# Taking early modes into x while the last weights load, and adding the late rows on two halves of the PE array

## Chip, cores, metric

The kernel runs on one core of a Trainium2 chip. Times are device microseconds (us) of that core, a median over executions. The profiler's span is about 2 us shorter than the time of the same execution, so spans are compared with spans and times with times. "Ratio" is the mean time of one kernel's fast runs over that of the other's fast runs of the same rounds, so it is not quite the ratio of the medians quoted.

## The reference, cut to what matters

An attention with forget gates gives x, of shape [8 batches, 576 rows, 512 columns]. Then comes a spectral mix:

```python
X = np.fft.rfft(x, axis=1)
# for the first 64 modes: complex weights, one 512 x 512 matrix per mode
Yr = einsum('bmd,mde->bme', Xr, w_r) - einsum('bmd,mde->bme', Xi, w_i)
Yi = einsum('bmd,mde->bme', Xr, w_i) + einsum('bmd,mde->bme', Xi, w_r)
y = np.fft.irfft(Y, n=576, axis=1)
u = x + y
out = u + np.maximum(u @ w_ch, 0.0)
```

The weights are 134 MB in DRAM, and loading them takes most of the time. y is an inverse transform: 128 numbers (64 modes, real and imaginary) per batch and column, times a fixed basis `BI`. Because the transform is linear, `u @ w_ch` can be built as `x @ w_ch` (called XW and computed while the weights load) plus the basis times `Y @ w_ch`.

## The kernel before

The weights come in tiles. The second half of the load uses tiles of 2 modes. The last 8 tiles that arrive hold the first 16 modes, so 32 of the 128 rows of Y are "late". After the last tile, each output job adds in PSUM, on PE: XW through an identity matrix, x also through the identity in jobs of type N, and the basis times `yy` (t=0 is Y, t=1 is `Y @ w_ch`) over all 128 rows.

```python
def emit_late(q4):     # late rows of four batches at once: 4 x 32 rows
    ... 4 transposes into ply, 4 matmuls with w_ch into plw
def emit_rows(b, pl):  # used for batch 0 only: straight to rows 0..31
    rows = slice(32 * (b % 4), 32 * (b % 4) + 32)
    nc.vector.tensor_copy(yy[0:32, b, 0, :], pl[0][rows, :])
    nc.scalar.copy(yy[0:32, b, 1, :], pl[1][rows, :])
def emit_late_rows(q4, pl):   # other batches: copy out, then move the rows by DMA
    nc.vector.tensor_copy(yl[:, 0, :], pl[0][:, :])
    nc.scalar.copy(yl[:, 1, :], pl[1][:, :])
    for j in range(1 - q4, 4):
        nc.sync.dma_start(yy[0:32, 4*q4 + j, :, :], yl[32*j : 32*j + 32, :, :])
def emit_x(job):       # identity matmuls: XW always, x for types N and Q
    for p, t in ((pu, x_all), (pz, XW)):
        if t is x_all and ty not in "NQ": continue
        for i in range(nb):
            nc.tensor.matmul(p[:, i, :], lhsT=ident_bf[:, :], rhs=t[...], start=True, stop=False)
def emit_out(job, ps, last):
    ... nc.tensor.matmul(p[:, i, :], lhsT=BI[:, block], rhs=yy[:, b, t, :])   # 128 rows
    # types N, Q: ACT copies pu out; P, W: DVE adds x to pu
    # types P, Q: ACT relu(pz), POOL adds; N, W: DVE max and add
    ... store
jobs = [(*j, ty) for j, ty in zip(jobs, "NPWPNPWPNNPWPNNPWNNN")]
```

There are 20 jobs: 16 of two 128-row blocks, and every fifth one (sb=4) of one block made of the last 64 rows of two batches. PSUM holds four tiles of two banks, and a job takes two of them (pu and pz).

The softmax here doesn't subtract the row's maximum and nothing guards it: scores larger than these inputs give would overflow.

Of the kernel before, what the change touches and what calls it, by code (L numbers as in the profile page):

```python
# [8 lines left out]
F32 = mybir.dt.float32  # L9
BF16 = mybir.dt.bfloat16  # L10
# [5 lines left out]
def _strided(ap: bass.AP, free_dims, offset_elems: int = 0) -> bass.AP:  # L16
    new_ap = [list(ap.ap[0])] + [list(x) for x in free_dims]
    return bass.AP(tensor=ap.tensor, offset=ap.offset + offset_elems, ap=new_ap)
# [3 lines left out]
def kernel(  # L22
# [11 lines left out]
    nc = tc.nc  # L34
    B, H, S, Dh = q.shape
    NM = moe_w_r.shape[0]
    D = H * Dh
# [4 lines left out]
    SP = NSB * 128  # L42
    NDC = D // 128
# [8 lines left out]
    def xi(b, sb):  # L52
        return (b % 2) * 3 + sb if sb < 3 else 6 + b % 2 if sb == 3 else 8
# [6 lines left out]
    const = ctx.enter_context(tc.tile_pool(name="const", bufs=1))  # L60
    xpool = ctx.enter_context(tc.tile_pool(name="xpool", bufs=1))
    wpool = ctx.enter_context(tc.tile_pool(name="wpool", bufs=NRING))
    xtpool = ctx.enter_context(tc.tile_pool(name="xtpool", bufs=3))
    x_all = xpool.tile([128, B // 2, NX, D], BF16, name="x_all")
    Yacc = xpool.tile([128, NDC, NM, 2 * B], F32, name="Yacc")
    late = {}
# [2 lines left out]
    wch = const.tile([128, NDC, D], BF16, name="wch")  # L69
    bas = const.tile([128, NSB + 1, NM, 2], BF16, name="bas")  # L70
    BI = const.tile([128, SP], BF16, name="BI")

    wtiles = {}

# [2 lines left out]
    NT = NDC * NG  # L77
    NTH = NT // 2
    M2 = MG // 2
    GL = 8  # L80

    def tile_of(n):
        if n < NTH:
# [33 lines left out]
    def emit_modes(n):  # L117
# [28 lines left out]
        if n < NG:  # L146
            nc.vector.tensor_copy(ysl, A[:, :, :, :])
        elif n < NTH:
            nc.vector.tensor_tensor(ysl, A[:, :, :, :], ysl, ALU.add)
        else:  # L150
            n8 = nm * 2
            yt, w = (late["YTl"], GL * n8) if g < GL else (late["YT"], 2 * NM)
            nc.vector.tensor_tensor(  # L153
                _strided(
                    yt[:, 0, 0, g * n8 : g * n8 + 1], [[B * w, NDC], [w, B], [1, n8]]
                ),
                _strided(A[:, 0, 0, 0:1], [[nm * 2 * B, NDC], [1, B], [B, n8]]),
                _strided(
                    Yacc[:, 0, g * nm, 0:1], [[NM * 2 * B, NDC], [1, B], [B, n8]]
                ),  # L160
                ALU.add,
            )

    with ExitStack() as actx:
# [191 lines left out]
        def emit_basis():  # L356
# [42 lines left out]
            for sc in range(NSB):  # L399
                bip = psT.tile([128, 128], F32, tag="tr", name="bip")  # L400
                nc.tensor.transpose(
                    bip[:, :],
                    Zt[:, sc, :, :].rearrange("p m ri -> p (m ri)"),
                    ident_f[:, :],
                )
                nc.vector.tensor_scalar(
                    BI[:, sc * 128 : (sc + 1) * 128], bip[:, :], coef[:], None, ALU.mult
                )


        QT, vaugs = {}, {}
# [177 lines left out]
        nmode = 0  # L589
# [41 lines left out]

    with ExitStack() as bctx:
        bsb = bctx.enter_context(tc.tile_pool(name="bsb", bufs=1))
        YT = bsb.tile([128, NDC, B, 2 * NM], BF16, name="YT")
        raw = xtpool.tile([128, NM, 3 * B], BF16, tag="XT3", name="YTl")
        nl = 2 * GL * M2
        YTl = (
            raw[:, :, :]
            .rearrange("p m c -> p (m c)")[:, 0 : NDC * B * nl]
            .rearrange("p (e b c) -> p e b c", e=NDC, b=B)  # L640
        )
        late["YT"], late["YTl"] = YT, YTl
        XW = bsb.tile([128, B // 2, NX, D], BF16, name="XW")
        yy = bsb.tile([128, B, 2, D], BF16, name="yy")
        nc.vector.memset(YT[:, :, :, 0 : 2 * GL * M2], 0.0)

        yflat = yy[:, :, :, :].rearrange("p b t e -> p (b t e)")
        xTs = [
            yflat[:, i * NDC * SP : (i + 1) * NDC * SP].rearrange(
                "p (e s) -> p e s", e=NDC  # L650
            )
            for i in range(3)
        ]

        with ExitStack() as cctx:
            late["psM"] = cctx.enter_context(
# [29 lines left out]
                        )  # L686
                    nc.scalar.copy(XW[:, bp, i0 + i, :], pxw[:, :])  # L687

            def emit_y(b):
                pyw = psBig.tile([128, D], F32, tag="big", name="pyw")  # L690
                for eb in range(NDC):
                    nc.tensor.matmul(  # L692
                        pyw[:, :],
                        lhsT=YT[:, eb, b, :],
                        rhs=wch[:, eb, :],
                        start=(eb == 0),
                        stop=(eb == NDC - 1),
                    )
                nc.scalar.copy(yy[:, b, 1, :], pyw[:, :])  # L699
                yp = psBig.tile([128, D], BF16, tag="big", name="yp")  # L700
                for eb in range(NDC):
                    nc.tensor.transpose(
                        yp[:, eb * 128 : (eb + 1) * 128], YT[:, eb, b, :], ident_bf[:, :]
                    )
                nc.vector.tensor_copy(yy[:, b, 0, :], yp[:, :])

            nx = ny = 0
            last = NT
            while nmode < last - 1:
                emit_modes(nmode)  # L710
                nmode += 1
                next_w()
                if nmode % 4 and nx < B:
                    emit_xw(nx)
                    nx += 1
                if nmode > last - 6 and ny < B - 1:
                    for _ in range(2 if ny < 4 else 1):
                        emit_y(ny)
                        ny += 1
            emit_y(ny)  # L720
            assert nx == B == ny + 1

        psZ = bctx.enter_context(
            tc.tile_pool(
# [3 lines left out]
        late["psM"], late["psZ"] = None, psZ  # L728


        def emit_late(q4):
            pl = psZ.tile([128, 2, D], F32, tag="z", name="pl")
            plw = pl[:, 0, :]
            ply = pl[:, 1, 0 : D // 2].bitcast(BF16)
            lhs = [
                YTl[:, eb, 4 * q4 : 4 * q4 + 4, :].rearrange("p b c -> p (b c)")
                for eb in range(NDC)
            ]
            for eb in range(NDC):
                nc.tensor.transpose(  # L740
                    ply[:, eb * 128 : (eb + 1) * 128], lhs[eb], ident_bf[:, :]
                )
            for eb in range(NDC):
                nc.tensor.matmul(
                    plw,
                    lhsT=lhs[eb],
                    rhs=wch[:, eb, :],
                    start=(eb == 0),
                    stop=(eb == NDC - 1),
                )  # L750
            return ply, plw

        yls = {}

        def emit_rows(b, pl):
            rows = slice(32 * (b % 4), 32 * (b % 4) + 32)
            nc.vector.tensor_copy(yy[0:32, b, 0, :], pl[0][rows, :])
            nc.scalar.copy(yy[0:32, b, 1, :], pl[1][rows, :])

        def emit_late_rows(q4, pl):  # L760
            yl = xtpool.tile([128, 2, D], BF16, tag="XT3", name="yl")
            nc.vector.tensor_copy(yl[:, 0, :], pl[0][:, :])
            nc.scalar.copy(yl[:, 1, :], pl[1][:, :])
            for j in range(1 - q4, 4):
                nc.sync.dma_start(
                    yy[0:32, 4 * q4 + j, :, :], yl[32 * j : 32 * j + 32, :, :]
                )

        def xblk(t, job):
            b, sb, nb, _ = job  # L770
# [21 lines left out]

        def emit_out(job, ps, last):
            b, sb, nb, ty = job
            for t, p in enumerate(ps):
                fresh = t == 0 and ty not in "NQ"
                for i in range(nb):
                    if sb == 4:
                        for h in range(2):
                            nc.tensor.matmul(  # L800
                                p[64 * h : 64 * h + 64, 0, :],
                                lhsT=BI[:, 512:576],
                                rhs=yy[:, b + h, t, :],
                                start=fresh,
                                stop=True,
                                skip_group_check=True,
                            )
                    else:
                        nc.tensor.matmul(
                            p[:, i, :],  # L810
                            lhsT=BI[:, (sb + i) * 128 : (sb + i + 1) * 128],
                            rhs=yy[:, b, t, :],
                            start=fresh,
                            stop=True,
                            skip_group_check=True,
                        )
            pu, pz = (p[:, 0:nb, :] for p in ps)
            uo = wpool.tile([128, 2, 2, D], F32, tag="wb", name="uo")
            u_sb, o_sb = uo[:, 0, 0:nb, :], uo[:, 1, 0:nb, :]
# [28 lines left out]
        for bp in range(B // 2):  # L848
            jobs += [(b, sb, 2) for b in (2 * bp, 2 * bp + 1) for sb in (0, 2)]
            jobs.append((2 * bp, 4, 1))  # L850
        jobs = [(*j, ty) for j, ty in zip(jobs, "NPWPNPWPNNPWPNNPWNNN")]
        ps0 = emit_x(jobs[0])
        emit_modes(nmode)
        pl = emit_late(0)
        emit_rows(0, pl)
        emit_late_rows(0, pl)
        for n, job in enumerate(jobs):
            emit_out(job, emit_x(job) if n else ps0, n == len(jobs) - 1)
            if n == 3:
                emit_late_rows(1, emit_late(1))  # L860
# [1 line left out]
_INS = ['q', 'k', 'v', 'f', 'moe_w_r', 'moe_w_i', 'moe_w_ch']  # L862
_OUTS = [((8, 576, 512), 'float32')]
# [25 lines left out]
```

## Time and profile before

| | before |
|---|---|
| time, median | 448.64 us (448.2 to 449.03), 3 runs |
| span of the profiled run | 446.5 us |
| last weights used | 405.34 us |
| tail after that | 41.2 us |

The strips of the page show each engine's busy share in 40 equal slices (in tenths), the clock granted to PE (in tenths), and the DMA share and rate.

```profile
PE   2388888989788788768597969999822238527993
...
PEclk9999999959599555897769578999955558856998
DMA  8999999999999999999999999999999999991698
GB/s 203 206 233 233 234 234 233 152 233 206 233 234 207 234 216 224 233 211 229 231 210 235 211 212 211 211 211 211 211 211 211 211 211 211 211 196 28 225 362 296
```

From about slice 26 the weight loads pace the kernel at 211 GB/s. PE has gaps there, and its clock is often at half. The last four slices are the tail.

The chain of waits gives the start of the tail. Its columns are start, duration, and what the chain went through.

```profile
405.34 0.56 PE A L138 x14
406.34 0.61 PE pl L740 x4
...
411.32 1.99 DMA yy<-yl
413.36 0.62 PE pu L809 x2
```

The last weights come at 405.34 us. The late rows follow. The DMA that moves them to other partitions takes 2 us from 411.32, and PE stands idle 1.4 us of it before the third job.

The next table is the tail by stage. Its columns are window, length, then busy time and count for PE, PE weight loads, DVE, ACT and POOL, then granted clock, DMA share and GB/s. The boundaries at 417, 424.2, 431.3 and 438.8 are close to the matmuls of the sb=4 jobs, so each of those stages is one group of five jobs.

```profile
core 0: us, PE busy (x) PEld busy (x) DVE busy (x) ACT busy (x) POOL busy (x), PEclk, DMA share, GB/s
406.30:408.90 2.60, 2.56 (x10) 1.18 (x11) 0.20 (x1) 0.00 (x0) 0.00 (x0) 0.50 0.00 0
408.90:412.50 3.60, 2.96 (x12) 0.95 (x10) 2.30 (x4) 3.00 (x4) 0.00 (x0) 1.00 0.00 0
412.50:417.00 4.50, 3.64 (x20) 1.71 (x20) 3.58 (x4) 1.03 (x1) 2.35 (x1) 1.00 0.57 201
417.00:424.20 7.20, 7.15 (x35) 2.86 (x36) 6.80 (x8) 4.03 (x5) 4.95 (x3) 1.00 0.64 232
424.20:431.30 7.10, 7.05 (x35) 2.77 (x34) 6.74 (x7) 3.54 (x4) 4.76 (x3) 1.00 0.97 347
431.30:438.80 7.50, 7.39 (x35) 2.96 (x34) 6.42 (x6) 3.37 (x4) 4.46 (x2) 1.00 0.99 368
438.80:446.50 7.70, 0.63 (x5) 0.14 (x4) 1.82 (x2) 0.85 (x2) 0.00 (x0) 0.77 0.73 275
```

A group takes 7.0 to 7.5 us with PE nearly full and DVE at 86 to 95%, and the DMA share is at 0.97 to 0.99 in the last two groups. The stage to 408.9 runs at half clock.

These PE lines of the timeline (start, busy time, line, operation) hold two durations that the costing needs.

```profile
416.61 0.38 PE L783 MATMUL pu<-x_all,ident_bf 128*128 128x512 bf16 x1
416.83 0.38 PE L783 MATMUL pz<-XW,ident_bf 128*128 128x512 bf16 x1
417.14 0.41 PE L800 MATMUL pu<-yy,BI 128*64 128x512 bf16 x2
417.38 0.38 PE L800 MATMUL pz<-yy,BI 128*64 128x512 bf16 x2
417.74 0.59 PE L783 MATMUL pz<-XW,ident_bf 128*128 128x512 bf16 x2
```

Full matmuls of 512 columns start 0.215 us apart. A job with sb=4 writes two halves of the columns of the array: a pair starts together (x2) and 0.24 us after the previous pair. From the full-array matmul at 416.83 to the first pair it is 0.31 us instead of 0.215, so about 0.09 us is added where the kind of tile changes. "Busy" in these lines is the pipelined length; the distance of the starts is what PE's time costs.

### The profile page before, as it was taken

What the parts mean: (1) busy time and instruction counts of PE and PEld (TensorE: products, weight loads), DVE (VectorE), ACT (ScalarE), POOL (GpSimd) and SP (SyncE); (2) the same over time, 40 slices, a digit from 0 to 9 for tenths busy, and PEclk for the clock granted to TensorE, in tenths of its full rate; (3) what the DMA queues carried; (4) which work ended last, traced back from release to release, by engine and by line L of the source; (5) the groups of instructions that cost most, each with busy time, mean ns of one, the idle gap of its engine ahead of it and who ended that gap; (6) DMA issues with size and microseconds to landing.
All of it is one profiled execution on the core that took longest, in us unless ns stands there. A gap on an engine that the chain in (4) does not pass through costs nothing.

```text
span 446.5 us, 11102 instructions
## 1 busy us (share of the span) xinstructions
PE 327.1 (73%) x4791; PEld 222.6 (50%) x4791; DVE 237.3 (53%) x602; ACT 202.4 (45%) x296; POOL 146.1 (33%) x194
## 2 busy tenths in 40 slices
PE   2388888989788788768597969999822238527993
PEld 1255555766566566556465746656612224323441
DVE  5768888776676546656377664223300002103894
ACT  3378888647567454664446533443200002102442
POOL 7333330534343323323333223232322323200661
PEclk9999999959599555897769578999955558856998
DMA  8999999999999999999999999999999999991698
GB/s 203 206 233 233 234 234 233 152 233 206 233 234 207 234 216 224 233 211 229 231 210 235 211 212 211 211 211 211 211 211 211 211 211 211 211 196 28 225 362 296
DMA packets 66431, 97.25 MB, mean 218 GB/s; under 512 B 3376, under 2 KB 44848, under 8 KB 66384
## 3 DMA queue, kind: packets, MB, share of 16 engines
q0 software_dynamic: 62480, 85.34, 103.3%
q1 hardware_dynamic: 3824, 11.09, 6.9%
q8 instruction: 37, 0.61, 0.5%
q10 hardware_dynamic: 80, 0.13, 0.1%
q14 instruction: 10, 0.08, 0.0%
HBM read 163.73 MB, written 9.44 MB: 388 GB/s over the span
## 4 chain that ended last, share of the span: by engine, by line
DMA 58%; PE 18%; DVE 7%; ACT 7%; issue 3%; POOL 1%; SPq 1%; DVEq 0%; ACTq 0%; POOLq 0%
DMA wb<-in_moe_w_i_dram 30%; DMA stk<-in_k_dram 13%; DMA stq<-in_q_dram 11%; ACT E L496 4%; DMA wb<-in_moe_w_r_dram 3%; PE tp L437 3%; PE pav L534 3%; PE pxw L680 3%; PE ps L489 3%; PE A L138 2%; DVE XT L581 2%; PE vp L461 1%; DVE uo L821 1%; PE ptr L669 1%; ACT KT L450 1%
## 5 line engine op out<-in xcount | busy, mean ns | idle before, releaser
L496 ACT ACTIVATE E<-ps 128x1024 bf16<-128x1024 f32 (+1 forms) x128 | 104.5, 859 | 39.3 <-PE ps L489 27.2
L138 PE MATMUL A<-XT,wb 128*128 128x16 bf16 x2048 | 71.6, 172 | 56.8 <-DMA wb<-in_moe_w_i_dram 35.0
L138 PEld LDWEIGHTS <-wb 128*128 128x128 bf16 x2048 | 64.0, 100 | 72.6 <-DMA wb<-in_moe_w_i_dram 38.2
L88 POOL DMA_DIRECT2D wb<-in_moe_w_r_dram x65 | 47.5, 731 | 134.7 <-PE A L138 30.4
L88 POOL DMA_DIRECT2D wb<-in_moe_w_i_dram x65 | 47.1, 725 | 78.2 <-DMA wb<-in_moe_w_i_dram 45.1
L489 PE MATMUL ps<-QTs,KT 64*128 64x64 bf16 (+4 forms) x384 | 57.5, 319 | 6.1 <-ACT E L496 5.9
L534 PE MATMUL pav<-va,E 128*128 128x65 bf16 (+1 forms) x1088 | 55.9, 210 | 4.3 <-DVE x_all L556 2.6
L534 PEld LDWEIGHTS <-E 128*128 128x128 bf16 (+1 forms) x1088 | 45.1, 114 | 15.8 <-issue 5.6
L153 DVE TENSOR_TENSOR YT<-A,Yacc 128x128 bf16<-128x128 f32 x24 | 8.9, 369 | 77.2 <-PE A L138 77.2
L511 DVE TENSOR_TENSOR E<-E,trimask 128x256 bf16<-128x256 bf16 (+2 forms) x128 | 38.2, 317 | 6.8 <-ACT E L496 6.4
L450 ACT COPY KT<-tp 128x640 bf16<-128x640 bf16 (+1 forms) x32 | 22.1, 745 | 26.6 <-PE tp L437 26.4
L687 ACT CAST XW<-pxw 128x512 bf16<-128x512 f32 x36 | 20.3, 587 | 29.8 <-PE pxw L680 25.1
L680 PE MATMUL pxw<-wch,yy 128*128 128x512 bf16 x144 | 33.5, 382 | 0.0
L699 ACT CAST yy<-pyw 128x512 bf16<-128x512 f32 x8 | 4.7, 586 | 60.7 <-PE pyw L692 60.7
L437 PE MATMUL tp<-ident_bf,kb 128*128 128x128 bf16 x144 | 16.1, 269 | 19.1 <-DVE kb L421 19.1
L556 DVE TENSOR_TENSOR x_all<-pav,rcp 128x384 bf16<-128x384 f32 x64 | 29.2, 456 | 0.9
L454 ACT COPY VT<-tp 128x640 bf16<-128x640 bf16 (+1 forms) x32 | 22.5, 753 | 12.6 <-PE tp L437 12.4
L489 PEld LDWEIGHTS <-KT 64*128 64x128 bf16 x384 | 18.1, 98 | 19.8 <-issue 11.6
L828 POOL TENSOR_TENSOR uo<-uo 128x1024 f32<-128x1024 f32 x7 | 16.5, 2359 | 29.3 <-DVE uo L821 25.5
L581 DVE CAST XT<-px 128x128 bf16<-128x128 f32 x32 | 21.0, 805 | 8.6 <-PE px L571 8.6
L425 DVE TENSOR_TENSOR vb<-stv,wdec 128x1152 bf16<-128x1152 f32 x16 | 21.6, 1351 | 5.4 <-PE tp L437 4.7
L452 DVE COPY QTs<-tp 128x640 bf16<-128x640 bf16 (+1 forms) x32 | 23.3, 767 | 0.8 <-PE tp L437 0.8
(108 smaller groups left out, 439.4 us busy)
## 6 DMA issues: line engine op xcount, KB each, us to landing
wb<-in_moe_w_r_dram POOLq DMA_DIRECT2D x63, 512.0 KB, 17.6
wb<-in_moe_w_i_dram POOLq DMA_DIRECT2D x63, 512.0 KB, 18.1
out_dram<-uo SPq DMA_DIRECT2D x16, 512.0 KB, 3.7
stv<-in_v_dram POOLq DMA_DIRECT2D x14, 576.0 KB, 15.6
stk<-in_k_dram POOLq DMA_DIRECT2D x16, 288.0 KB, 15.3
stq<-in_q_dram POOLq DMA_DIRECT2D x16, 288.0 KB, 15.3
stv<-in_v_dram SPq DMA_DIRECT2D x2, 576.0 KB, 6.1
out_dram<-uo SPq DMA_DIRECT2D x7, 128.0 KB, 3.9
```

Source lines behind the costliest of these rows:

```text
L88: tc.keep_in_program_order(nc.gpsimd.dma_start(dst, src))
L138: nc.tensor.matmul(A[:, eb, mi, :], lhsT=wb[:, t, mi, r * D + eb * 128 : r * D + (eb + 1) * 128], rhs=XT3[:, m, c0 : c0 + 2 * B], start=(i ...
L437: nc.tensor.transpose(tp[:, r - r0, :, :].rearrange("c h p -> c (h p)"), sb[:, r, :, :].rearrange("p b d -> p (b d)"), ident_bf[:, :],)
L450: nc.scalar.copy(rows(KTs[pr % 2][:, :, 0:S]), tv)
L452: nc.vector.tensor_copy(rows(QT[pr][:, :, :]), tv)
L489: nc.tensor.matmul(ps[:, b, o : o + n], lhsT=KTs[pr % 2][bs, h, jb * 128 : (jb + 1) * 128], rhs=QT[pr][bs, h, jb * 128 + c0 : jb * 128 + c ...
L496: nc.scalar.activation(E[:, :, piece * 512 : piece * 512 + w], ps[:, :, 0:w], ACT.Exp, scale=scale,)
L511: nc.vector.tensor_tensor(dg, dg, tr, ALU.mult)
L534: nc.tensor.matmul(pav[64 * half : 64 * half + w, slot, :], lhsT=E[:, b, c : c + (w - 1) * st + 1 : st], rhs=va[:, jb, b, :], start=(n == ...
L556: nc.vector.tensor_tensor(xo, pi, ri, ALU.mult)
L581: nc.vector.tensor_copy(_strided(XT3[:, 0, B + b : B + b + 1], [[3 * B, NM], [B, 2]]), px[:, :, :],)
L680: nc.tensor.matmul(pxw[:, :], lhsT=xT[:, eb, i * 128 : (i + 1) * 128], rhs=wch[:, eb, :], start=(eb == 0), stop=(eb == NDC - 1),)
```

## The change

The intent was to shrink the tail. Now 16 tiles (32 modes, 64 rows) are late instead of 8, but everything early is already added into x_all and XW while those 16 tiles load. Only 64 rows stay for the tail. The late rows of two batches fit on 128 rows, one batch on each half. No row has to move, and the matmuls for pu and pz can run at the same time, each on half of the rows of the array. `BIx` is the basis with its halves exchanged.

```diff
-    GL = 8
+    GL = 16
+    HM = 64
+            nc.sync.dma_start(BIx[0:HM, :], BI[HM:128, :])
+            nc.sync.dma_start(BIx[HM:128, :], BI[0:HM, :])
+        def y_rows(yt, l, bp, ply, plw):     # two batches: 4 transposes, 8 matmuls of 64 output rows
+            ...
+        def add_y(l, b, sb, pus, first=()):
+            for t, pu in enumerate(pus):
+                    half = (b + h + t) % 2       # pu and pz on opposite halves
+                    basis = BI if half != l else BIx
+                    nc.tensor.matmul(dst, lhsT=basis[hs, cs], rhs=yy[hs, l, b // 2, t, :], ...)
+            def emit_part(b, sb):                # one block, during the loads
+                ... x and XW through the identity into pu and pz
+                add_y(0, b, sb, (pu[:, :], pz[:, :]))
+                nc.vector.tensor_copy(x_all[:, at[0], at[1], :], pu[:, :])
+                nc.scalar.copy(XW[:, at[0], at[1], :], pz[:, :])
             while nmode < last - 1:
...
+                if nmode > last - GL:
+                    for _ in range(3):           # three blocks per weight tile
+                        if parts: ...
-        emit_late(0); emit_rows(0, pl); emit_late_rows(0, pl)   # and emit_late_rows(1, ...) after job 3
+        emit_late(0)
-        ... "NPWPNPWPNNPWPNNPWNNN"
+        ... "NPNPNQNPNNPNQNNPNNNN"
+            if n % 5 == 2 and n // 5 < B // 2 - 1:
+                emit_late(n // 5 + 1)
```

(emit_out now calls add_y, and emit_late calls y_rows for two batches.)

More of the change, by code (lines that the diff above doesn't have):

```diff
@@ L71 @@
     BI = const.tile([128, SP], BF16, name="BI")
+    BIx = const.tile([128, SP], BF16, name="BIx")
     wtiles = {}
@@ L151, in emit_modes @@
             n8 = nm * 2
-            yt, w = (late["YTl"], GL * n8) if g < GL else (late["YT"], 2 * NM)
+            yt = late["YTl"] if g < GL else late["YTe"]
+            c0 = g % GL * n8
             nc.vector.tensor_tensor(
                 _strided(
-                    yt[:, 0, 0, g * n8 : g * n8 + 1], [[B * w, NDC], [w, B], [1, n8]]
+                    yt[:, 0, 0, c0 : c0 + 1], [[B * HM, NDC], [HM, B], [1, n8]]
                 ),
@@ L633 @@
         bsb = bctx.enter_context(tc.tile_pool(name="bsb", bufs=1))
-        YT = bsb.tile([128, NDC, B, 2 * NM], BF16, name="YT")
-        raw = xtpool.tile([128, NM, 3 * B], BF16, tag="XT3", name="YTl")
-        nl = 2 * GL * M2
-        YTl = (
-            raw[:, :, :]
-            .rearrange("p m c -> p (m c)")[:, 0 : NDC * B * nl]
-            .rearrange("p (e b c) -> p e b c", e=NDC, b=B)
-        )
-        late["YT"], late["YTl"] = YT, YTl
+        YTe = bsb.tile([128, NDC, B, HM], BF16, name="YTe")
+        YTl = bsb.tile([128, NDC, B, HM], BF16, name="YTl")
+        late["YTe"], late["YTl"] = YTe, YTl
         XW = bsb.tile([128, B // 2, NX, D], BF16, name="XW")
-        yy = bsb.tile([128, B, 2, D], BF16, name="yy")
-        nc.vector.memset(YT[:, :, :, 0 : 2 * GL * M2], 0.0)
-        yflat = yy[:, :, :, :].rearrange("p b t e -> p (b t e)")
+        yy = bsb.tile([128, 2, B // 2, 2, D], BF16, name="yy")
+        yflat = yy[:, :, :, :, :].rearrange("p l b t e -> p (l b t e)")
         xTs = [
@@ L653 @@
         ]
+        def y_rows(yt, l, bp, ply, plw):
+            for eb in range(NDC):
+                nc.tensor.transpose(
+                    ply[:, eb * 128 : (eb + 1) * 128],
+                    _strided(yt[:, eb, 2 * bp, 0:1], [[1, 2 * HM]]),
+                    ident_bf[:, :],
+                )
+            for eb in range(NDC):
+                for h in range(2):
+                    nc.tensor.matmul(
+                        plw[HM * h : HM * h + HM, :],
+                        lhsT=yt[:, eb, 2 * bp + 1 - h, :],
+                        rhs=wch[:, eb, :],
+                        start=(eb == 0),
+                        stop=(eb == NDC - 1),
+                        skip_group_check=True,
+                    )
+            nc.vector.tensor_copy(yy[:, l, bp, 0, :], ply)
+            nc.scalar.copy(yy[:, l, bp, 1, :], plw)
+        def add_y(l, b, sb, pus, first=()):
+            for h in range(2 if sb == 4 else 1):
+                for t, pu in enumerate(pus):
+                    half = (b + h + t) % 2
+                    hs = slice(HM * half, HM * half + HM)
+                    basis = BI if half != l else BIx
+                    if sb == 4:
+                        dst, cs = pu[64 * h : 64 * h + 64, :], slice(512, 576)
+                    else:
+                        dst, cs = pu, slice(sb * 128, sb * 128 + 128)
+                    nc.tensor.matmul(
+                        dst,
+                        lhsT=basis[hs, cs],
+                        rhs=yy[hs, l, b // 2, t, :],
+                        start=t in first,
+                        stop=True,
+                        skip_group_check=True,
+                    )
         with ExitStack() as cctx:
@@ L687, in emit_xw, with emit_y @@
                     nc.scalar.copy(XW[:, bp, i0 + i, :], pxw[:, :])
-            def emit_y(b):
+            def emit_y(bp):
                 pyw = psBig.tile([128, D], F32, tag="big", name="pyw")
-                for eb in range(NDC):
-                    nc.tensor.matmul(
-                        pyw[:, :],
-                        lhsT=YT[:, eb, b, :],
-                        rhs=wch[:, eb, :],
-                        start=(eb == 0),
-                        stop=(eb == NDC - 1),
-                    )
-                nc.scalar.copy(yy[:, b, 1, :], pyw[:, :])
-                yp = psBig.tile([128, D], BF16, tag="big", name="yp")
-                for eb in range(NDC):
-                    nc.tensor.transpose(
-                        yp[:, eb * 128 : (eb + 1) * 128], YT[:, eb, b, :], ident_bf[:, :]
-                    )
-                nc.vector.tensor_copy(yy[:, b, 0, :], yp[:, :])
-            nx = ny = 0
+                yp = psBig.tile([128, D], BF16, tag="big", name="yp")
+                y_rows(YTe, 0, bp, yp[:, :], pyw[:, :])
+            def emit_part(b, sb):
+                pu = psBig.tile([128, D], F32, tag="big", name="pu0")
+                pz = psBig.tile([128, D], F32, tag="big", name="pz0")
+                at = b // 2, xi(b, sb)
+                for p, t in ((pu, x_all), (pz, XW)):
+                    nc.tensor.matmul(
+                        p[:, :],
+                        lhsT=ident_bf[:, :],
+                        rhs=t[:, at[0], at[1], :],
+                        start=True,
+                        stop=False,
+                        skip_group_check=True,
+                    )
+                add_y(0, b, sb, (pu[:, :], pz[:, :]))
+                nc.vector.tensor_copy(x_all[:, at[0], at[1], :], pu[:, :])
+                nc.scalar.copy(XW[:, at[0], at[1], :], pz[:, :])
+            parts = []
+            for bp in range(B // 2):
+                parts += [(bp, None)]
+                parts += [(b, sb) for b in (2 * bp, 2 * bp + 1) for sb in range(4)]
+                parts += [(2 * bp, 4)]
+            nx = 0
             last = NT
@@ L715 @@
                     nx += 1
-                if nmode > last - 6 and ny < B - 1:
-                    for _ in range(2 if ny < 4 else 1):
-                        emit_y(ny)
-                        ny += 1
-            emit_y(ny)
-            assert nx == B == ny + 1
+                if nmode > last - GL:
+                    assert nx == B
+                    for _ in range(3):
+                        if parts:
+                            a, sb = parts.pop(0)
+                            emit_y(a) if sb is None else emit_part(a, sb)
+            assert not parts
         psZ = bctx.enter_context(
@@ L728, with emit_late @@
         late["psM"], late["psZ"] = None, psZ
-        def emit_late(q4):
+        def emit_late(bp):
             pl = psZ.tile([128, 2, D], F32, tag="z", name="pl")
-            plw = pl[:, 0, :]
-            ply = pl[:, 1, 0 : D // 2].bitcast(BF16)
-            lhs = [
-                YTl[:, eb, 4 * q4 : 4 * q4 + 4, :].rearrange("p b c -> p (b c)")
-                for eb in range(NDC)
-            ]
-            for eb in range(NDC):
-                nc.tensor.transpose(
-                    ply[:, eb * 128 : (eb + 1) * 128], lhs[eb], ident_bf[:, :]
-                )
-            for eb in range(NDC):
-                nc.tensor.matmul(
-                    plw,
-                    lhsT=lhs[eb],
-                    rhs=wch[:, eb, :],
-                    start=(eb == 0),
-                    stop=(eb == NDC - 1),
-                )
-            return ply, plw
-        yls = {}
-        def emit_rows(b, pl):
-            rows = slice(32 * (b % 4), 32 * (b % 4) + 32)
-            nc.vector.tensor_copy(yy[0:32, b, 0, :], pl[0][rows, :])
-            nc.scalar.copy(yy[0:32, b, 1, :], pl[1][rows, :])
-        def emit_late_rows(q4, pl):
-            yl = xtpool.tile([128, 2, D], BF16, tag="XT3", name="yl")
-            nc.vector.tensor_copy(yl[:, 0, :], pl[0][:, :])
-            nc.scalar.copy(yl[:, 1, :], pl[1][:, :])
-            for j in range(1 - q4, 4):
-                nc.sync.dma_start(
-                    yy[0:32, 4 * q4 + j, :, :], yl[32 * j : 32 * j + 32, :, :]
-                )
+            y_rows(YTl, 1, bp, pl[:, 1, 0 : D // 2].bitcast(BF16), pl[:, 0, :])
         def xblk(t, job):
@@ L794, in emit_out @@
             b, sb, nb, ty = job
-            for t, p in enumerate(ps):
-                fresh = t == 0 and ty not in "NQ"
-                for i in range(nb):
-                    if sb == 4:
-                        for h in range(2):
-                            nc.tensor.matmul(
-                                p[64 * h : 64 * h + 64, 0, :],
-                                lhsT=BI[:, 512:576],
-                                rhs=yy[:, b + h, t, :],
-                                start=fresh,
-                                stop=True,
-                                skip_group_check=True,
-                            )
-                    else:
-                        nc.tensor.matmul(
-                            p[:, i, :],
-                            lhsT=BI[:, (sb + i) * 128 : (sb + i + 1) * 128],
-                            rhs=yy[:, b, t, :],
-                            start=fresh,
-                            stop=True,
-                            skip_group_check=True,
-                        )
+            for i in range(nb):
+                add_y(
+                    1, b, sb + i, [p[:, i, :] for p in ps], () if ty in "NQ" else (0,)
+                )
             pu, pz = (p[:, 0:nb, :] for p in ps)
@@ L850 @@
             jobs.append((2 * bp, 4, 1))
-        jobs = [(*j, ty) for j, ty in zip(jobs, "NPWPNPWPNNPWPNNPWNNN")]
+        jobs = [(*j, ty) for j, ty in zip(jobs, "NPNPNQNPNNPNQNNPNNNN")]
         ps0 = emit_x(jobs[0])
         emit_modes(nmode)
-        pl = emit_late(0)
-        emit_rows(0, pl)
-        emit_late_rows(0, pl)
+        emit_late(0)
         for n, job in enumerate(jobs):
             emit_out(job, emit_x(job) if n else ps0, n == len(jobs) - 1)
-            if n == 3:
-                emit_late_rows(1, emit_late(1))
+            if n % 5 == 2 and n // 5 < B // 2 - 1:
+                emit_late(n // 5 + 1)
 _INS = ['q', 'k', 'v', 'f', 'moe_w_r', 'moe_w_i', 'moe_w_ch']
```

## The prediction

> **What bounds it now.** Two stages. In the strips by slice and the chain of waits, weight loading paces everything from about 288 to 405 us: a 2-mode tile arrives every 4.97 us, and PE works about 1.2 us per tile at granted clock 0.50. The last weights are used at 405.34 us; the span ends at 446.5. So 41.2 us are a tail. In the timeline it has a slow start (first output matmul 409.16, PE idle 411.9 to 413.35 waiting for the SBUF-to-SBUF copy that shifts late rows; first store issued 413.2), then four groups of five output jobs, 7.1 us per group (the sb=4 matmuls start at 417.14, 424.16, 431.28, 438.81). Per group DVE has about 6.8 us (1.22, 1.22+1.23, 1.22, 1.23, 0.69) and PE 6.7 us (0.215 us per 512-column matmul, start to start); stores move 2.36 MB at about 370 GB/s, 6.4 us. Last DVE 440.92, then about 5.6 us for the last stores.
>
> **During the loads.** Added per tile: three blocks, each two identity matmuls, one half-K pair and two copies of about 0.6 us. PE: 3 x (2 x 0.215 + 0.22 + 2 x 0.093) = 2.5 us warm, under 4.6 cold, plus 1.2: it fits in about 5 us, with nine weight buffers of slack, and is done one tile before the end. The last weights should still arrive at about 405. Free, and no gain.
>
> **The tail: removed.** The seven yl-to-yy copies and their wait (about 1.5 us at the start, 4.3 us of SyncE issue); half of PE's y matmuls: half-row pairs start 3 to 6 ns apart and take 0.22 us together (scores in attention show it), 0.43 before; four W jobs' additions and some P's: DVE falls from about 27 to 22 us.
>
> **The tail: added.** Jobs that load x on PE rise from 9 to 15 (+0.43 us each, +2.6); three more late y groups in the loop (about 1.2 us each, one existed); 53 changes between full and half-array matmuls instead of 7. The Trainium skill (TensorEngine Tiling (Array Packing), Key Properties) says that changing tiling mode drains PE; this trace agrees: a change costs about 93 ns over the normal spacing (128-column transpose to half-row score: 151 ns against about 55). Summing: PE 28.3 us after the last mode before, 32.2 after. ACT rises to 23 us.
>
> A second cost: pu and pz now finish together, later in the job, so an N job holds its pz tile for about 3.6 us (matmuls 1.0, wait 0.2, ACT copy 1.02, DVE 1.23); four PSUM tiles hold two jobs, so N after N cannot go faster than about 1.8 us (1.73 before), and late tiles take a slot. Estimate: groups of 8 to 9 us where a late group lies, 7.3 in the last; PE ends at 441 to 444.
>
> The stores are no longer backed up, so the end after the last DVE shrinks from 5.6 to about 4 us. Early gain about 1.5 to 2 us, end 1.5, loop loss 3 to 5: about even.
>
> **Predicted: 449.0 us, 8 in 10 between 443.5 and 454.** Faster by over 2%: 0.05; within 2%: 0.91; slower by over 2%: 0.04.
>
> **Right or wrong shows in:** last weights used at 405 +- 1; first store about 1 us earlier; no yl copies; pairs 0.22 us, switches about 0.09 us in PE's spacing; PE or PSUM releases (waits of PE on ACT/DVE) pacing the loop, DVE under 85%; store share under 0.95.
>
> **What would make it wrong:** PE has slack through PSUM slots freed sooner than I walked: then stores bound it (25.5 us from about 412.5) and about 442 comes out; parts late and the last modes delayed; long PSUM stalls: 455.

## The result and the profile after

| | before | after |
|---|---|---|
| time, median of 4 runs | 448.83 us (448.2 to 449.25) | 451.12 us (450.71 to 451.28) |
| ratio | | 1.0053 (95%: 1.0039 to 1.0068) |
| span, profiled run | 446.5 us | 449.5 us |
| last weights used | 405.34 us | 405.30 us |
| sb=4 matmuls of the four groups start at | 417.14, 424.16, 431.28, 438.81 | 417.18, 425.99, 434.63, 442.13 |
| end of the last DVE instruction | 440.92 us | 444.82 us |

The change is a small loss, 0.5%. The strips of the kernel after:

```profile
PE   2388888979789859859597779999467988958994
...
PEclk9999999959697696897669959999769888876998
DMA  8999999999999999999999999999999999991677
GB/s 206 206 239 233 233 233 233 153 233 207 233 233 207 233 226 214 233 221 219 233 218 225 212 212 210 211 211 211 211 211 211 211 211 211 211 171 49 248 275 273
```

PE is much busier in the slices with the loads, and the loads run at the same 211 GB/s. The last two slices move 275 and 273 GB/s, where the kernel before had 362 and 296.

The tail of the kernel after by stage (columns as before; the groups end at 426, 434.6 and 442.2):

```profile
406.30:408.90 2.60, 2.60 (x13) 1.01 (x14) 0.10 (x1) 0.00 (x0) 0.00 (x0) 0.50 0.00 0
408.90:412.50 3.60, 3.44 (x11) 1.02 (x10) 1.06 (x2) 2.30 (x3) 0.00 (x0) 0.50 0.00 0
412.50:417.00 4.50, 4.35 (x26) 1.27 (x26) 3.53 (x5) 2.13 (x4) 2.36 (x1) 1.00 0.32 122
417.00:426.00 9.00, 8.24 (x53) 2.53 (x52) 4.35 (x5) 6.01 (x8) 5.89 (x3) 1.00 0.70 264
426.00:434.60 8.60, 8.12 (x48) 2.46 (x48) 4.60 (x5) 5.88 (x8) 4.62 (x3) 1.00 0.77 293
434.60:442.20 7.60, 7.05 (x37) 1.94 (x36) 5.20 (x5) 4.44 (x6) 3.60 (x2) 1.00 0.68 254
442.20:449.50 7.30, 0.99 (x5) 0.23 (x5) 2.03 (x3) 1.35 (x2) 0.00 (x0) 0.80 0.76 288
```

Three things are to be read here. Up to 417 us nothing is won (a later run with full clock there does win up to 1 us). The groups take 8.8, 8.6 and 7.5 us (differences of the sb=4 starts) where 7.0, 7.1 and 7.5 stood. DVE's share of a group falls from 86 to 95% to 48 to 68%, and the store share falls below 0.8. So the engine that was relieved was one of two that were near full, and PE, the other, now has more to do.

PE lines of the timeline in the tail after, a P job between full-array matmuls:

```profile
415.57 0.60 PE L796 MATMUL pz<-XW,ident_bf 128*128 128x512 bf16 x2
416.11 0.39 PE L683 MATMUL pu<-yy,BIx 64*128 64x512 bf16 x1
416.11 0.39 PE L683 MATMUL pz<-yy,BI 64*128 64x512 bf16 x1
416.33 0.38 PE L683 MATMUL pu<-yy,BIx 64*128 64x512 bf16 x1
416.34 0.38 PE L683 MATMUL pz<-yy,BI 64*128 64x512 bf16 x1
416.65 0.39 PE L796 MATMUL pu<-x_all,ident_bf 128*128 128x512 bf16 x1
```

The half-row pair for pu and pz starts together, and the next pair 0.22 us later: the two halves do run at the same time. But it is 0.31 us from the full matmul to the first pair (415.80 to 416.11), and 0.31 from the last pair to the full matmul (416.34 to 416.65). Nearly every job pays this on the way in and on the way out: of the 48 changes of tile kind at full clock in this tail, 39 take 90 to 104 ns more than the normal spacing, and the others are longer, by waits or by a record that is missing. Not every y matmul found its partner: 8 of the 64 (without the sb=4 jobs) ran with none at full clock, four of them in the first P job.

I split PE's time from the first late transpose to the start of the last matmul. Each matmul is counted with its full-clock spacing (0.216 us for 512 columns, 0.056 for 128, a concurrent partner 0), and each change of tile kind is given up to 0.093 us. What exceeds this by more than 0.03 us is waits and half clock. Smaller leftovers are in no column.

| | length, us | matmuls | changes: number, us | waits and half clock |
|---|---|---|---|---|
| before | 32.7 | 27.4 | 7, 0.65 | 4.5 |
| after | 36.5 | 25.6 | 53, 4.9 | 5.3 |

The saving in matmuls is 1.8 us only, because six more jobs load x through PE (2.6 us, as an experiment below shows) and two more late groups (the transposes and w_ch matmuls of one emit_late) are in the tail. (Three of the 186 matmul records of this tail are missing from the trace after; their time falls to the last column.) The changes of tile kind take 4.3 us more. The 0.093 per change is an assignment here; the experiments test it.

The start of the tail was expected to gain and didn't. Timeline lines of the kernel before (engine, line, operation):

```profile
408.69 0.41 DVE L757 COPY yy<-pl 32x512 bf16<-32x512 bf16 x1 [2.41 <-PE pl L744]
...
409.16 0.59 PE L809 MATMUL pu<-yy,BI 128*128 128x512 bf16 x2
...
410.83 1.22 DVE L830 SCALAR_TENSOR_TENSOR uo<-pz,uo 128x1024 f32<-128x1024 f32 x1 [0.60 <-ACT uo L823]
...
413.21 0.58 SPq L840 DMA_DIRECT2D out_dram<-uo  x1
...
413.36 0.60 PE L809 MATMUL pu<-yy,BI 128*128 128x512 bf16 x2 [1.42 <-DMA yy<-yl]
```

and of the kernel after:

```profile
408.69 1.03 PE L796 MATMUL pz<-XW,ident_bf 128*128 128x512 bf16 x2
...
409.66 0.60 PE L683 MATMUL pu<-yy,BI 64*128 64x512 bf16 x1
...
411.77 1.23 DVE L825 SCALAR_TENSOR_TENSOR uo<-pz,uo 128x1024 f32<-128x1024 f32 x1 [2.54 <-PE pz L683]
...
413.02 0.37 SPq L835 DMA_DIRECT2D out_dram<-uo  x1
```

The copies through DMA are gone, so SyncE can issue the first store as soon as it is ready. But the first output is ready about 0.9 us later (DVE at 411.77 instead of 410.83): the first y matmul starts 0.5 us later, and the clock stays at half until 412.5 us where it became full at 408.9. The first store is issued at 413.02 instead of 413.21.

### The profile page after: what moved, and what is told of

Same layout as the page of the kernel before. It is cut to its first block, busy times and chain, and to the rows that moved or that the text cites. A ratio compares the mean times of both kernels' runs of the same rounds, so it can differ in the third digit from the quotient of the medians.

```text
span 449.5 us, 11520 instructions
## 1 busy us (share of the span) xinstructions
PE 352.9 (79%) x4955; PEld 220.9 (49%) x4971; DVE 252.9 (56%) x628; ACT 227.4 (51%) x335; POOL 145.9 (32%) x194
## 4 chain that ended last, share of the span: by engine, by line
DMA 66%; PE 14%; ACT 7%; DVE 3%; issue 3%; POOL 1%; DVEq 0%; ACTq 0%; POOLq 0%
DMA wb<-in_moe_w_i_dram 50%; DMA wb<-in_moe_w_r_dram 11%; DMA stk<-in_k_dram 5%; ACT E L501 4%; PE tp L442 2%; PE ps L494 2%; PE pav L539 2%; PE pz L796 1%; PE pu L683 1%; PE pl L662 1%; ACT uo L818 1%; PE A L140 1%; DVE uo L825 1%; PE pu L796 1%; ACT KT L455 1%
## 5 line engine op out<-in xcount | busy, mean ns | idle before, releaser
L140 PE MATMUL A<-XT,wb 128*128 128x16 bf16 x2048 | 70.2, 171 | 30.0 <-DMA wb<-in_moe_w_i_dram 21.3
L140 PEld LDWEIGHTS <-wb 128*128 128x128 bf16 x2048 | 62.3, 98 | 45.4 <-DMA wb<-in_moe_w_i_dram 23.4
L494 PE MATMUL ps<-QTs,KT 64*128 64x64 bf16 (+4 forms) x384 | 56.6, 312 | 6.3 <-ACT E L501 6.1
L539 PE MATMUL pav<-va,E 128*128 128x65 bf16 (+1 forms) x1088 | 54.1, 206 | 5.3 <-DVE x_all L561 3.5
L539 PEld LDWEIGHTS <-E 128*128 128x128 bf16 (+1 forms) x1088 | 43.6, 111 | 16.7 <-issue 6.5
L746 ACT CAST XW<-pz 128x512 bf16<-128x512 f32 x36 | 21.1, 585 | 34.5 <-PE pz L683 34.2
L745 DVE CAST x_all<-pu 128x512 bf16<-128x512 f32 x36 | 24.9, 692 | 20.0 <-PE pz L683 12.3
L717 PE MATMUL pxw<-wch,yy 128*128 128x512 bf16 x136 | 31.8, 379 | 1.3 <-issue 1.2
L442 PE MATMUL tp<-ident_bf,kb 128*128 128x128 bf16 x144 | 15.2, 258 | 19.4 <-DVE kb L426 19.4
L156 DVE TENSOR_TENSOR YTe<-A,Yacc 128x128 bf16<-128x128 f32 x16 | 5.9, 371 | 43.1 <-PE A L140 43.1
## 6 DMA issues: line engine op xcount, KB each, us to landing
wb<-in_moe_w_r_dram POOLq DMA_DIRECT2D x63, 512.0 KB, 17.3
```

The lines of the kernel that those rows point to most:

```text
L140: nc.tensor.matmul(A[:, eb, mi, :], lhsT=wb[:, t, mi, r * D + eb * 128 : r * D + (eb + 1) * 128], rhs=XT3[:, m, c0 : c0 + 2 * B], start=(i ...
L442: nc.tensor.transpose(tp[:, r - r0, :, :].rearrange("c h p -> c (h p)"), sb[:, r, :, :].rearrange("p b d -> p (b d)"), ident_bf[:, :],)
L494: nc.tensor.matmul(ps[:, b, o : o + n], lhsT=KTs[pr % 2][bs, h, jb * 128 : (jb + 1) * 128], rhs=QT[pr][bs, h, jb * 128 + c0 : jb * 128 + c ...
L539: nc.tensor.matmul(pav[64 * half : 64 * half + w, slot, :], lhsT=E[:, b, c : c + (w - 1) * st + 1 : st], rhs=va[:, jb, b, :], start=(n == ...
L717: nc.tensor.matmul(pxw[:, :], lhsT=xT[:, eb, i * 128 : (i + 1) * 128], rhs=wch[:, eb, :], start=(eb == 0), stop=(eb == NDC - 1),)
L745: nc.vector.tensor_copy(x_all[:, at[0], at[1], :], pu[:, :])
```

## The experiments

The theory (A) is that PE paces the tail after the change: changes of tile kind and added x loads eat what the halves save, while DVE and the stores get slack that nobody uses. The rivals are: (B) the time that jobs hold PSUM, or ACT, paces the tail, and PE's spacing doesn't matter; (C) the block updates during the loads disturb the loads or the last modes; (D) the late clock explains the loss.

Each round ran beside the kernel before on the same chip; ratios are to it. The kernel after stands at 1.0053.

### Old job types

```diff
-        ... "NPNPNQNPNNPNQNNPNNNN"
+        ... "NPWPNPWPNNPWPNNPWNNN"
```

> The changed kernel with the job types of the kernel before (7 P, 4 W, 5 N among the full jobs, no Q): six jobs fewer load x through PE. Theory A (PE paces the tail through array mode changes and added x loads): PE has about 2.6 us less work in the tail, but DVE's work rises from about 22 to about 29 us, so DVE takes over the pace; about 450 us, between 448.5 and 451.5. Rival B (the tail is paced by how long an N or Q job holds its PSUM tiles, or by ACT): fewer N and Q jobs free PSUM earlier, ACT falls by about 7 us, and the time drops to about 446 to 448. Rival C (the blocks during the loads disturb the end): no change, 451.

Measured: 450.73 us, ratio 1.0061 (1.0044 to 1.0077), the same as the kernel after. PE's tail is 35.3 us, 1.2 less than after, but hardly any of it reached the end (span 449.0 against 449.5). B's 446 to 448 did not come. C's "no change" would fit as well; the next run decides that one.

### No block updates

```diff
-                            emit_y(a) if sb is None else emit_part(a, sb)
+                            emit_y(a) if sb is None else None
```

> The changed kernel without the 36 block updates during the loads (the result is wrong on purpose: the early modes' y is left out; the y and y@w_ch groups themselves stay). Theory A: the updates are free, so the last weights are still used at about 405.3 us and the time stays 451 within 1 us; PE's clock at the start of the tail may differ. Rival C (the updates delay the last modes or the loads): the time falls by 1 us or more and the last weights are used earlier.

Measured: 451.11 us, ratio 1.0060 (1.0045 to 1.0075). From 360 to 380 us PE was busy 4.8 us instead of 17.3, at the same 1.12 DMA share, and nothing came of it: the last weights were used at 405.73 us, no earlier than the 405.30 of the kernel after. The updates are free, and C falls. The result is wrong, yet the comparison with the reference passed: what is left out is too small for its tolerance, so "correct" means little for this part in the other runs, too.

### The kernel before with the new types

```diff
-        ... "NPWPNPWPNNPWPNNPWNNN"
+        ... "NPNPNQNPNNPNQNNPNNNN"
```

> The kernel before with the job types of the changed one (9 N, 5 P, 2 Q among the full jobs). Theory A: six more x loads on PE add 2.6 us of PE work to a tail in which PE and DVE were both near full, DVE falls by about 6 us: PE paces, plus 1.5 to 3 us, about 451 (450 to 452.5). Rival B (DVE alone paced the kernel before): faster than 448.8 by 1 to 3 us.

Measured: 449.43 us, ratio 1.0028 (1.0013 to 1.0043), which is 1.2 us more than the 448.25 of the same rounds and a little under the expected range of the increase. PE's matmuls rise by 2.6 us to 30.0, and its tail by 1.3 us. Relieving DVE at PE's cost wins nothing here.

### Late y on the full array

```diff
+    BZ = const.tile([128, 2, SP], BF16, name="BZ")     # basis with one half zero
-                        lhsT=basis[hs, cs],
-                        rhs=yy[hs, l, b // 2, t, :],
+                        lhsT=BZ[:, half, cs] if l else basis[hs, cs],
+                        rhs=yy[:, l, b // 2, t, :] if l else yy[hs, l, b // 2, t, :],
```

> The changed kernel, but the late y matmuls of the output jobs use all 128 rows of the array, with a basis whose other half is zero (same results). Mode changes in the tail fall from 53 to about 10; each full job has 4 y matmuls one after the other (0.86 us) in place of two pairs (0.44 us). Theory A at 93 ns per change and 0.215 us per matmul: minus about 4 us of changes, plus about 16 x 0.42 + 1 = 7.7 us of matmuls: PE paces fully, time up by about 3 us to 454 (452.5 to 456). A rival in which mode changes cost nothing would have +7 us (458); a rival in which PE has slack in the tail would have no change (451).

Measured: 457.62 us, ratio 1.0213 (1.0196 to 1.023). This equals the "changes cost nothing" rival in the number, but for another reason. I filled BZ right behind the copies that make BIx, and DVE waited for them. The DVE line of the timeline shows it:

```profile
25.39 0.32 DVE L418 COPY BZ<-BIx 64x640 bf16<-64x640 bf16 x1 [5.37 <-DMA BIx<-BI]
```

DVE sat idle 5.4 us near the start, everything after it moved, and the first late transpose came at 412.85 instead of 406.30 us. Its time says nothing about the tail. It was repeated with the fill after the attention stage:

> The zero-padded full-array basis again, now filled after the attention stage: in the first try the fill waited for a copy near the start of the program and the last weights were used 6.5 us late (412.8 instead of 406.3 us for the first late transpose), so its 457.6 us told nothing of the tail; its tail alone, from the first late transpose to the last matmul, lasted 36.7 us against 36.5 of the changed kernel. Theory A: with the loads on time again the whole is within 1 us of the changed kernel, 451 (450 to 452.5): what the half-row pairs save in matmuls (about 6.7 us) goes to mode changes (about 3.4) and to waits. If the pairs were a clear gain, this kernel would be 454 or more.

Measured: 452.07 us, ratio 1.0082 (1.0067 to 1.0097), as A expected. PE's tail is 36.8 us: 32.4 of matmuls, 17 changes, 2.5 of waits and half clock. With twice the y matmuls the tail is only 0.3 us longer than in the kernel after. The halves save 6.7 us of matmuls and give back 3.3 in changes and 2.8 in waits and half clock. But the clock was not the same: here it was full from 410.5 us, 3.3 us into the tail, and in the kernel after only 6.2 us into it. The tail also began later, at 407.20 us, so the 452.07 is no clean measure either. A fairer measure is the stretch from the first sb=4 matmul to the last, which has full clock in both: 25.74 us here (and in the first try), 24.95 in the kernel after. So as a whole the two halves are worth about 0.8 us there.

### More changes of tile kind

```diff
-                for i in range(nb):
+                for i in range(nb) if blocks is None else blocks:   # emit_x: block 0 only
             for i in range(nb):
+                if i and job is not jobs[0]:
+                    emit_x(job, ps, (i,))       # block 1's x right before its y
                 add_y(
```

> The changed kernel with the same matmuls, but the x loads of a job's second block stand between the y pairs of its first and second block: 87 mode changes in the tail instead of 53. Theory A at 93 ns each: 34 x 0.093 = 3.2 us more PE time; some of it hides in waits for PSUM, so plus 2 to 3.2 us, about 453.7 (453 to 454.5). If mode changes cost the time nothing (they hide behind ACT, DVE or the stores): 451 within 0.7.

Measured: 457.53, 453.07, 453.08 and 456.75 us, in two groups. The lower group is what A expects. The profiled run is of the upper one; its stages show why it is no test of the changes alone:

```profile
410.00:415.00 5.00, 5.00 (x14) 0.91 (x10) 2.36 (x2) 2.50 (x3) 1.20 (x1) 0.50 0.27 107
415.00:420.00 5.00, 5.00 (x19) 1.38 (x18) 1.65 (x2) 1.00 (x2) 1.14 (x1) 0.50 0.50 205
```

PE counts as busy without a gap from 410 to 420 us and yet has half clock there; in this run the clock became full only at 421.6 us. So the clock is a second effect that has to be held still. After that the clock is full, and from the first sb=4 matmul to the last it took 26.93 us.

### Fillers that keep PE busy before the tail

```diff
+                if nmode > last - 3:        # behind the two tiles before the last
+                    fl = psBig.tile([128, D], F32, tag="big", name="fl")
+                    with tc.issue_after(late["mm"].ins):
+                        for r in range(8):
+                            nc.tensor.matmul(fl[:, :], lhsT=ident_bf[:, :],
+                                             rhs=x_all[:, 0, r % NX, :], start=True, stop=True, ...)
```

> The changed kernel with 8 matmuls of no use behind each of the last two waits for weights, so that PE stays busy and its clock may be full when the tail begins (in the changed kernel the clock was at half until 412.5 us, in the kernel before until 408.9). Theory A: in the cold part of the tail PE has about 3 us of work at half speed; full clock from 405 saves 1 to 2 us: about 449.5 (448.5 to 450.3). If the start of the tail is paced by the chain through DVE and ACT copies alone: 451 within 0.5. If the fillers delay the last modes: later than 451.

Measured: 449.38 us, ratio 1.0022 (1.0007 to 1.0036). The stages of warm_after show full clock from the beginning of the tail:

```profile
405.00:410.00 5.00, 4.51 (x56) 2.11 (x54) 0.79 (x2) 1.44 (x2) 0.00 (x0) 1.00 0.00 0
410.00:415.00 5.00, 4.82 (x28) 1.51 (x28) 4.01 (x4) 2.78 (x4) 2.30 (x1) 1.00 0.28 110
```

PE's tail shrinks from 36.5 to 34.4 us, and its waits and half clock from 5.3 to 3.0. For a fair comparison the kernel before got fillers too (6 and 1 of them, since its y work already stands in that place):

> The kernel before with filler matmuls behind the last two waits for weights, nothing else. In the kernel before the clock was at half from 406.3 to 408.9 us, with about 2.5 us of PE work in it: full clock saves 0.6 to 1.3 us: 447.5 (447.0 to 448.0). Then the change compared at full clock (warm_after against warm_before) is a loss of about 2 us (1.4 to 2.4).

Measured: 447.18 us, ratio 0.9962 (0.9947 to 0.9977): the time is in its range, but by the ratio the fillers save 1.7 us, more than expected. Kernel after against kernel before with fillers in both: 1.0022 / 0.9962 = 1.006, within noise the same as the 1.0053 without, and by the ratios 2.7 us, a little above the 1.4 to 2.4 expected. So D falls as the cause of the loss. The traces show where the loss is. The tail starts at 406.62 us in warm_after and at 406.68 in warm_before. At full clock the first sb=4 matmul comes at 415.45 against 416.43, so the change does win up to 1 us early (one trace each, and warm_before's is of its slowest execution, 0.6 us over its median). From there to the last sb=4 matmul it takes 24.95 us against 21.67, the same lengths as without fillers. The first and the last of these matmuls in warm_before:

```profile
416.43 0.41 PE L812 MATMUL pu<-yy,BI 128*64 128x512 bf16 x2
...
438.10 0.41 PE L812 MATMUL pu<-yy,BI 128*64 128x512 bf16 x2
```

and in warm_after:

```profile
415.45 0.40 PE L683 MATMUL pu<-yy,BI 64*64 64x512 bf16 x1
...
440.41 0.40 PE L683 MATMUL pu<-yy,BI 64*64 64x512 bf16 x1
```

Then the dose of changes again, with fillers:

> split_jobs (87 mode changes in the tail) with the filler matmuls of warm_after: the dose of mode changes again, with the clock out of the way. split_jobs without fillers fell into two groups, 453.1 and 456.8 to 457.5 us, and in the profiled one of 457.5 the clock stayed at half until 421.6 us. Theory A: at full clock 34 more changes at 93 ns are 3.2 us, some hidden in waits: 451.4 to 452.6 against 449.4 of warm_after, and one group only. If mode changes are free: 449.4 within 0.6.

Measured: 452.36, 456.51, 455.83 and 455.29 us; ratio 1.0135 (1.0096 to 1.0174). The profiled run is the 452.36, with full clock from 405.5. In it 87 changes stand against 53 of warm_after, and PE's tail is 37.4 us against 34.4: 2.95 us for 34 changes, 87 ns each. This doesn't rest on my assignment, but it is a net figure of one trace: the new order also left three fewer pairs together (0.65 us), and waits shrank by 1.3 us. From the first sb=4 matmul to the last, 26 changes more took 2.2 us more here (27.13 against 24.95) and 2.0 in the profiled split_jobs. So the spacing of PE does reach the end, and B falls. The expectation of one group only failed: three runs are 3 to 4 us slower, at about the same mean clock (0.858 to 0.863), and only the fast one has a trace. What those three lost stays open.

### Batch 1's late rows written directly

```diff
         emit_rows(0, pl)
+        emit_rows(1, pl)
-            for j in range(1 - q4, 4):
+            for j in range(2 if q4 == 0 else 0, 4):
```

In the kernel before this takes away the wait at 413.36; once alone and once with fillers.

> The kernel before with the late rows of batch 1 written directly, without fillers. The wait of 1.6 us for the copy goes, DVE has 0.4 and ACT 0.6 us more: minus 0.4 to 1.2 us, about 447.6 (447.0 to 448.2). Together with warm_before it should add up to the 1.55 us of rows1_warm.

Measured: 448.03 us, ratio 0.9979 (0.9962 to 0.9996). In its profiled run the clock became full only at 411.5 us, where it was 408.9 in the kernel before, so it does not show the direct writing alone.

> The kernel before, with two small changes: the late rows of batch 1 are written straight from PSUM to rows 0 to 31 by DVE and ACT, as those of batch 0 are, so that the third job needs no copy by DMA (its wait was 1.6 us); and filler matmuls behind the last waits for weights, so that the clock is full when the tail begins. Theory A: the wait goes (minus 1.6, plus 0.4 of DVE), the cold part saves up to 1; but DVE, near 95% busy, and the stores pace the rest: 446.5 (445.5 to 447.8). If DVE and stores alone set the end: 448.5 within 0.5.

Measured: 446.84 us (446.59 to 446.91), ratio 0.9964 (0.9949 to 0.9979). It beats both kernels, but it is no better than the fillers alone (0.9962), so the two gains don't add in the time. Its stages near the end have the stores at a share of about 1, which suggests (argued, not tested) that the stores set the end there:

```profile
425.00:430.00 5.00, 4.89 (x25) 1.98 (x23) 4.79 (x5) 2.81 (x3) 2.82 (x2) 1.00 1.00 383
430.00:435.00 5.00, 5.00 (x26) 2.12 (x23) 4.61 (x5) 2.12 (x3) 3.90 (x2) 1.00 1.02 406
435.00:440.00 5.00, 2.76 (x14) 0.86 (x12) 3.43 (x4) 2.11 (x3) 0.37 (x1) 1.00 0.98 360
```

### Q jobs made P, with fillers

```diff
-        ... "NPNPNQNPNNPNQNNPNNNN"
+        ... "NPNPNPNPNNPNPNNPNNNN"
```

> warm_after with the two Q jobs made P (x added by DVE instead of PE and ACT): PE has 0.86 us less, ACT 2.0 us less, DVE 2.4 us more of its free time. Theory A (PE and the PSUM held behind it pace the tail): 448.7 (448.0 to 449.2). If DVE already paced it: 449.4 or more.

Measured: 448.49 us, ratio 0.9990 (0.9975 to 1.0005). By the ratios (0.9990 against 1.0022) that is 1.4 us faster than warm_after, though DVE has more to do: giving work back from PE and ACT to DVE helps. This is the best that I got out of the changed kernel, and it only reaches the kernel before, which has no fillers; with them that one stands at 0.9962.

### Not tried

Loading x and XW through the identity on halves as well would leave PE in one kind of tile and remove most changes. Both halves would have to add into one PSUM bank. What the change would be worth without changes of tile kind is open.

## Why the prediction was right or wrong

It was right in the whole: 449.0 predicted with 443.5 to 454 as the range, 451.12 measured, and within 2%. The range is wide, and the point is 2.1 us off: a loss of 2.3 us where next to none was predicted. Point by point:

- **The loads:** right. The last weights were used at 405.30 us, and no_parts2 shows the updates to be free.
- **Pairs and changes:** right. Pairs start 0.22 us apart; a change costs 90 to 104 ns by the spacing, and 87 net by the dose test.
- **The loop loss of 3 to 5 us:** right. From the first sb=4 matmul to the last it took 21.67 us before and 24.95 after, plus 3.3 us, all at full clock. The groups were 8.8, 8.6 and 7.5 us, where 8 to 9 and 7.3 were predicted. PE's last matmul started at 442.79 (441 to 444 predicted). DVE was at 48 to 68% and the store share at 0.68 to 0.77 in the groups.
- **What paces the loop:** PE first, then waits. Split as in the table of PE's time, the 3.3 us are 1.3 less of matmuls, 3.0 more of changes (38 instead of 6), 1.3 more of waits (2.4 instead of 1.15) and 0.3 of small leftovers; these are the figures of warm_after, whose loop is as long and whose trace lacks no record. The waits that the profile of the kernel after names are for ACT and DVE to empty PSUM tiles, 1.3 us in its tail. The new job types alone make the loop of the kernel before 1.8 us longer (23.43 us in before_newtypes2). The prediction's sum for PE in the whole tail, 28.3 to 32.2, was about 1 us too high (28.1 to 30.9 by the traces of before and warm_after), and waits, which it named but did not add up, made up for it: that part of the hit is luck. How much of the waits is ACT's pace and how much the PSUM held is not separated.
- **"Early gain about 1.5 to 2 us", "first store about 1 us earlier":** wrong, and this is the term that was mis-sized. The first group's sb=4 matmul came at 417.18 against 417.14: no gain. The wait for the copies did go, but the first output came 0.9 us later and the first store only 0.2 us earlier, and PE's clock stayed at half 3.6 us longer than before. The prediction says nothing of the clock in the tail. With full clock in both kernels the gain is up to 1.0 us (415.45 against 416.43), so the clock took up to 1 us of it, and the rest, to 1.5 or 2, is missing at full clock, too. Why the clock came later is open.
- **"End 1.5" us gained:** from the last DVE instruction to the end it was 5.58 us before and 4.64 after, so 0.94.

With 0 in place of 1.5 to 2 and 0.94 in place of 1.5, the sum of the prediction's own terms is a loss of about 2 to 4 us; measured are 3.0 in span and 2.3 in time. Two statements of the Trainium skill bear on this. TensorEngine Tiling (Array Packing), section Key Properties, says that changing the tiling mode drains PE; the trace agrees, with about 0.09 us each. TensorE: Matmul & The Clock Gate, section Part 1: The HAM clock gate, says that the clock becomes full after at least one busy window of about 3.4 us, of windows that run on without regard to the program. The kernel after does not decide it: PE counted as busy 6.0 of 6.2 us from 406.3 to 412.5, all at half clock, which need hold no more than one whole window. split_jobs does not agree: PE counted as busy from 410 to 420 us without a gap, and the clock became full at 421.6. "Busy" is what the records say; how much of the array worked they do not show.

## What to carry to other kernels

When two engines are both near full, taking work off one and giving some to the other can lose, as it did here; add up both before choosing. Count the changes of tile kind as well: with one on either side of two half-array pairs, the two changes of 0.09 us cost nearly what one pair saves (how longer runs of pairs fare was not tested). Work put into the loading stage was free here, and so were matmuls of no use that keep PE's clock full for the tail: they gave 0.3 to 0.4%, and the change itself gave nothing. When the clock differs between two runs, compare a stretch in which it is full in both.

## What the Trainium skill lacked or had wrong

- TensorEngine Tiling (Array Packing) says that a mode change drains PE but gives no figure. Here it was 90 to 104 ns by the spacing of starts (39 of 48 changes at full clock in the kernel after), for row halves as for column halves, and 87 ns net in the time of PE (34 more changes, 2.95 us).
- TensorE: Matmul & The Clock Gate gives one busy window of about 3.4 us as enough for full clock. In split_jobs the records show PE busy 5.00 of 5.00 us twice in a row (410 to 420 us) at clock 0.50, and the clock became full at 421.6 us. How half-array matmuls and changes count for the clock is on no page that I read.
